# One core, attention and two expert layers: the gated sums are put together in another row, the weight work is spread one block a step, and two experts' second layer is turned

## The chip, the cores and the metric

The kernel runs on one core of one Trainium2 chip. The metric is the device time of one execution in microseconds (us). Three runs of the kernel before gave 814.67, 816.64 and 810.50 us, a median of 814.67. One profiled execution took 813.66 us; its trace spans 811.8 us from the first to the last instruction, with a granted TensorE clock of 0.996 on average.

## The reference

Three layers follow one another, all in fp32 and with outputs of 2304 tokens x 512:

```
x   = windowed attention(q, k, v)                     # 4 x 8 heads, 576 tokens, window 128, slopes on |i-j|
x   = (sigmoid(x @ w_gate) * (x @ w_val)) @ w_out     # 512 -> 1536 -> 512
idx = argmax(cosine(x, expert_emb) / tau)             # one of 8 experts a token
out[mask] = gate_w * (relu(x @ w1[e]) @ w2[e])        # 512 -> 1024 -> 512, for the tokens of expert e
```

## The kernel before, in words

An fp32 value is split in a high and a low part, and a product is three matmuls: high x high, low x high, high x low. The high part is a cast on ACT (`hi_copy`, L105), the low part a subtraction on DVE (`lo_sub`, L121).

**The gated layer.** The 512 -> 1536 product with the gate and value weights is done by Strassen's scheme for pairs of 512 tokens. The second pair (pair 1) is a loop of 12 steps f (L838 to L872), one block of 128 hidden rows a step. In a step PE runs seven products of six matmuls each, with names m1 to m7 and PSUM banks a, b and c, in this order: m5 (left operand S1, into c), m6 (S2, a), m1 of the next step (A11, a), m7 (S3, a), m2 of the next step (A12, b), m4 (A22, a), m3 (S4, c). Bank a has two buffers, so each product into it waits for an ACT copy of an earlier one: `r` at L535 and `c` at L527, L538 and L542. The sums of banks are made on DVE (L531, L539, L549). The same 512 x 512 tokens are later multiplied with w_out in Strassen's form too, so `keep_g` (L452 to L475) makes from four gated blocks (two steps f, an even and an odd one) the three of them that are used alone (A11, A12, A22) and the sums S1 to S4, and sends each by a DMA that POOL issues (L461) to DRAM. The gated value itself is the STT of L458 (a SCALAR_TENSOR_TENSOR on DVE), a sum is a TENSOR_TENSOR at L464. An even and an odd step share one tile `gq` with two halves, `low` and `high`.

**w_out's blocks.** w_out comes as 64-bit floats, 12 blocks of 128 rows (`wor`, 512 KB each, loaded by SP at L749). `split64` (L137) turns a block to fp32 in a row `cvwo`: one ACT instruction (L125), three on DVE (L131, L132, L134), a POOL DMA to DRAM (L141), then the cast on ACT (L105, named `wo`) and the subtraction on DVE (L121). A table WO_AT says in which step of pair 1 which block is converted.

**The rows of w_out and the route.** Then five rows of tokens (L1317, index i) go through w_out (`mm2`, L919), with Strassen's product in the middle. After each row the route to the experts is made: TensorE turns the rows, DVE copies them (`xT`, L960), TensorE multiplies with the expert vectors (`part`, L966; `lp`, L974). In rows i = 2 and 3 the weights of expert 0 are loaded and split (L1354 and L1355, tiles `wer`, `weh`, `wel`, eight parts).

**The experts.** The loop from L1431 runs experts 1 to 7. `ffn1` (L1121) makes the hidden rows with the weights stationary and the tokens moving; CAPS gives the columns: 384, 384, 384, 352, 320, 288, 256, 256 for e = 0 to 7. `ffn2` (L1139) has 128 tokens of the hidden rows as the stationary operand and moves 512 columns of weights, 24 matmuls for each tile of tokens; the last tile of e = 4 has 64 tokens, that of e = 5 has 32. DVE scales by the gate (L1143) and POOL scatters the rows to `out` (L1144). Between the tiles TensorE turns the gathered tokens of the next expert (`tx`, L1101, four transposes a tile).

**What sets the order.** Each engine has one queue and runs it in order. The order in a queue is set by a planner from modelled times, not by the program's text; a wait at the head of a queue holds everything behind it. Tiles of the kernel are rows of pools (33 rows in `bpool`, 10 in `mid`); a row that is used again waits for its last reader, a DMA too.

Of the kernel before, what the change touches and what calls it, by code (L numbers as in the profile page):

```python
# [9 lines left out]
F32 = mybir.dt.float32  # L10
# [50 lines left out]
def attn_ffn_moe(ctx: ExitStack, tc: tile.TileContext, qkd, vd, wgv, w_out, emb, tau, w1, w2, cst, ids, out):  # L61
# [381 lines left out]
        nc.sync.dma_start(gT_d[f * P:(f + 1) * P, t0:t0 + n], gate)  # L443

    NAMES = ["A11", "A12", "A22", "S1", "S2", "S3", "S4"]
    gq = {}

    def g7_rows(name, kk, n=1):
        r = (NAMES.index(name) * KF // 2 + kk) * P
# [2 lines left out]
    def keep_g(f, half, gate, val):  # L452
        kk, odd = divmod(f, 2)
        if not odd and kk not in gq:
            gq[kk] = slot([P, 2, 512], F32, f"gq{kk}")
        low, high = gq[kk][:, 0, :], gq[kk][:, 1, :]
        o = gate if odd else (low, high)[half]
        nc.vector.scalar_tensor_tensor(out=o, in0=gate, scalar=1.0, in1=val, op0=ALU.add, op1=ALU.mult)  # L458

        def put(name, t):  # L460
            nc.gpsimd.dma_start(g7_rows(name, kk), t)  # L461

        def sums(name, t, x, y, op):
            nc.vector.tensor_tensor(out=t, in0=x, in1=y, op=op)  # L464
            put(name, t)

        if odd or not half:
            put(f"A{half + 1}{odd + 1}", o)
        if not odd and not half:
            sums("S3", high, high, low, ALU.subtract)  # L470
        elif odd and half:
            sums("S2", high, o, high, ALU.add)
            sums("S1", low, high, low, ALU.add)
        elif odd:
            sums("S4", val, o, high, ALU.subtract)  # L475

    def piece(mm, ev):
        def both():
# [266 lines left out]
    def load_wo(j):  # L745
        if j >= KF:
            return
        t = slot([P, 1024], I32, f"wor{j}")
        nc.sync.dma_start(t, w_out[j].bitcast(I32))  # L749
        wo_raw[j] = t  # L750
# [57 lines left out]
    run(2)  # L808
    load_wt(1)
    load_wo(0)  # L810

    g_t = {}
    NB2 = 5
# [20 lines left out]
    sv[0]["m2"]()  # L834
    bB["S3+"]()
    bB["S3"]()
    WO_AT = {1: [0], 2: [1], 3: [2], 4: [3, 4], 5: [5], 6: [6], 7: [7, 8], 8: [9], 9: [10], 10: [11]}
    for f in range(KF):  # L838
        s, t = sv[f], sv[f + 1] if f + 1 < KF else None
        s["m5"]()  # L840
        if f == 0:
            bB["A22"]()
            bB["S4+"]()
        if f + 1 < NC:
            sum_w(f + 1, store=False)
        split_w(1, f + 1, 0)
        s["m6"]()
        if f == 0:
            bB["S4"]()
        if t:  # L850
            t["m1"]()
        s["m7"]()
        split_w(1, f + 1, 1)
        if t:
            t["m2"]()
        load_wt(f + 2)
        s["m4"]()
        for j in WO_AT.get(f, []):
            split_wo(j)
        for j in WO_AT.get(f + 2, []):  # L860
            load_wo(j)
        if f == KF - 1:
            split_g(ROWS[0], [0, 1])
        s["m3"]()
        if f == KF - 2:
            load_g(ROWS[0])
        if f == 7:
            load_emb()
        elif f == 9:
            norm_emb()  # L870
        elif f == 10:
            turn_emb()  # L872
# [257 lines left out]
    def ffn2(e, t, u, hs, idx, w=P):  # L1130
# [3 lines left out]
        for k in range(KE):  # L1134
# [3 lines left out]
            for h, ww in ((hh, wh), (hl, wh), (hh, wl)):  # L1138
# [5 lines left out]
        nc.gpsimd.indirect_dma_start(out=out, out_offset=IOA(ap=idx[0:w], axis=0), in_=y[0:w, :], in_offset=None,  # L1144
                                     bounds_check=NT - 1, oob_is_err=False)

    def tok_a(e, t):
        xh, xl = xe.pop(e)
        hr = op_.tile([P, FE], F32, tag="c", name=f"hr{e}_{t}")
        for z in range(2):  # L1150
            m = pt("s", f"ht{e}_{t}_{z}", 2)
            ds = slice(z * 512, (z + 1) * 512)
            cnt = 0
            for k in range(KD):
                wh, wl = wset[e][k]
                for x, w in ((xh, wh), (xl, wh), (xh, wl)):
                    nc.tensor.matmul(m, x[:, k, :], w[:, ds], start=(cnt == 0), stop=(cnt == 3 * KD - 1))
                    cnt += 1
            nc.scalar.activation(out=hr[:, ds], in_=m, func=AF.Relu)
        return hr  # L1160
# [142 lines left out]
    def sums_w2(lo, hi):  # L1303
        for kk in range(lo, hi):
# [5 lines left out]
            (1, 1): [lambda: sums_w2(3, 4), lambda: split_op(0)], (1, 2): [lambda: sums_w2(4, 5)],  # L1310
            (1, 3): [lambda: load_op(1), lambda: sums_w2(5, 6), lambda: split_w2(5), lambda: split_op(1)]}

    def more(i, z):
        for t in MORE.get((i, z), []):
            t()

    for i, b in enumerate(ROWS):  # L1317
        inner = {}
        if i == STRASSEN_AT:
            inner = strassen(late)  # L1320
        m = [pt("m", f"y{b}_{u}", 3) for u in range(2)]
        mm2(b, 0, 0, 4, m[0])
        if i and i != STRASSEN_AT:
            route_a(ROWS[i - 1], *late)
        for t in inner.get(0, []):
            t()
        more(i, 0)
        mm2(b, 0, 4, KF, m[0])
        for t in inner.get(1, []):
            t()  # L1330
        more(i, 1)
        mm2(b, 1, 0, 4, m[1])
        if i and i != STRASSEN_AT:
            route_b(ROWS[i - 1])
        for t in inner.get(2, []):
            t()
        more(i, 2)
        mm2(b, 1, 4, MT, m[1])
        if b == LATE[0]:
            close()  # L1340
        if b == LATE[1]:
            make_x(0, CE * P, True)
            for t in range(CE):
                transp(0, t, t)
        for t in inner.get(3, []):
            t()
        mm2(b, 1, MT, KF, m[1])
        if i + 1 < NB2 and i + 1 != STRASSEN_AT:
            split_g(ROWS[i + 1])
        if i >= STRASSEN_AT and i + 2 < NB2:  # L1350
            load_g(ROWS[i + 2])
        more(i, 3)
        late = route_x(b, m)
        for j in {2: (0, 1, 2, 3), 3: (4, 5, 6, 7)}.get(i, ()):  # L1354
            split_we(0, j, load_we(0, j), "a", "v")  # L1355

    def weights(e, lo=0, hi=NP):
        for j in range(lo, hi):
# [61 lines left out]
    def load_part(e, lo, hi):  # L1420
        if e < E:
            for j in range(lo, hi):
                raws[e, j] = load_we(order[e], j, e)
# [4 lines left out]

    gathers(2)
    load_part(2, 0, KD)  # L1430
    for e in range(1, E):  # L1431
        if e + 1 == E:
            tc.keep_in_program_order(nc.gpsimd.drain())
        load_part(e + 1, KD, NP)
        inner = {j + 1: [lambda e=e, j=j: convert(e + 1, j)] for j in range(KD)}
        if e == 1:
            inner[1].insert(0, lambda: ffn2(0, CE, 0, rest, col(0, CE)))
        t0 = EARLY[e] if e < len(EARLY) else 0
        hs = ffn1(e, CAPS[e] - t0 * P, between=inner)
        load_part(e + 2, 0, KD)  # L1440
        if e + 1 < E:
            make_x(e + 1, CAPS[e + 1])
        later = list(range(KD, NP))
        for t in tiles(e):
            if e + 1 < E and t in tiles(e + 1):
                transp(e + 1, t, t, width(e + 1, t))
            if t == tiles(e)[-1]:
                gathers(e + 2)
            if t >= t0:
                for j in later[:2]:  # L1450
                    convert(e + 1, j)
                later = later[2:]
                with tc.issue_after(latest(ENG.PE)[0]) if e + 1 == E else nullcontext():
                    ffn2(e, t, t - t0, hs, col(e, t), width(e, t))
# [117 lines left out]
```

## Time and profile before

| what | number |
|---|---|
| median of three runs | 814.67 us (810.50 to 816.64) |
| profiled execution, and its span | 813.66 us, 811.8 us |
| PE busy | 787.8 us, 97% of the span |
| DVE, ACT, POOL busy | 565.9 us (70%), 448.9 us (55%), 205.6 us (25%) |
| DMA over the span | 205 GB/s |
| stages: attention and first pair; pair 1; rows of w_out and Strassen; experts | to about 262; 262 to 392; to 555; to 812 us |

PE is busy 97% of the time, so a change counts through the gaps between matmuls and the number and spacing of the matmuls. Matmuls overlap: a row of the timeline shows the start and the duration of an instruction, and the spacing of starts is what a matmul costs PE; its duration is longer. Brackets give the idle time before an instruction and what ended it.

### The profile page before, as it was taken

To read this page: it belongs to the slowest core of one execution; us is meant where nothing else is said; L and a number is where in the kernel's file an instruction comes from. 1 tells how busy PE (TensorE), PEld (TensorE's weight loads), DVE (VectorE), ACT (ScalarE), POOL (GpSimd) and SP (SyncE) were. 2 spreads that over 40 slices of the span, in tenths; PEclk is the share of its full clock that TensorE was granted. 3 is DMA by queue.
4 is the path that set the end of the run, shared out by engine and by line. 5 is a ranking of instruction groups with operands and counts; after the bars stand their busy time and mean duration, and the time that the engine had idled before them with its cause. 6 is when DMAs were issued, how large, how long until landed. Compare 5 with 4: busy or idle time off the path is not lost. (4 is left out here: it accounts for less than half of the span.)

```text
span 811.8 us, 15640 instructions
## 1 busy us (share of the span) xinstructions
PE 787.8 (97%) x5562; PEld 652.3 (80%) x5563; DVE 565.9 (70%) x1430; ACT 448.9 (55%) x946; POOL 205.6 (25%) x330
## 2 busy tenths in 40 slices
PE   9989999999999999999999999999999999999997
PEld 5767878878888787778778877768789989879896
DVE  7988977777789887788679666746647554465621
ACT  6888766666556555456466587645445433344510
POOL 6856423322000022222310202422223021110200
PEclk9999999999999999999999999999999999999999
DMA  8687467765565789889946692232578364445100
GB/s 271 188 268 229 156 230 258 234 210 204 184 245 196 290 299 329 314 306 325 349 108 202 232 338 83 99 143 79 167 266 280 132 224 158 152 163 202 56 23 18
DMA packets 71070, 166.61 MB, mean 205 GB/s; under 512 B 9511, under 2 KB 23591, under 8 KB 70992
## 3 DMA queue, kind: packets, MB, share of 16 engines
q1 hardware_dynamic: 61136, 136.08, 50.1%
q0 software_dynamic: 9856, 29.53, 10.1%
q8 instruction: 44, 0.72, 0.4%
q14 instruction: 34, 0.28, 0.1%
HBM read 116.20 MB, written 50.03 MB: 205 GB/s over the span
## 5 line engine op out<-in xcount | busy, mean ns | idle before, releaser
L1121 PE MATMUL h<-xe,weh 128*128 128x256 f32 (+4 forms) x512 | 105.6, 300 | 0.2 <-DVE h L1124 0.2
L117 POOL TENSOR_SCALAR p<-p,rs 128x192 f32<-128x192 f32 x140 | 75.5, 557 | 103.7 <-DVE rs L268 53.3
L1139 PE MATMUL z<-weh,h 128*128 128x512 f32 (+3 forms) x320 | 101.5, 396 | 0.0
L121 DVE TENSOR_TENSOR wel<-wer,weh 128x1024 fp32r<-128x1024 f32 x64 | 77.1, 1220 | 18.3 <-ACT weh L105 6.1
L1121 PEld LDWEIGHTS h<-xe,weh 128*128 128x128 f32 x512 | 83.8, 189 | 1.7 <-DVE h L1124 0.8
L919 PE MATMUL y<-wo,gh 128*128 128x512 f32 x240 | 78.5, 399 | 0.0
L105 ACT CAST weh<-wer 128x1024 fp32r<-128x1024 f32 x64 | 66.5, 1048 | 21.3 <-DMA wer<-in_w 10.2
L252 ACT ACTIVATE p<-p,mx 128x192 f32<-128x192 f32 x144 | 64.0, 446 | 24.9 <-DVE mx L249 24.6
L1121 PE MATMUL h<-xe,wel 128*128 128x256 f32 (+4 forms) x256 | 76.6, 299 | 0.0
L1123 ACT ACTIVATE h<-h 128x256 fp32r<-128x256 f32 (+4 forms) x64 | 26.7, 417 | 79.3 <-PE h L1121 74.9
L1139 PEld LDWEIGHTS z<-weh,h 128*128 128x128 f32 (+3 forms) x320 | 56.4, 180 | 14.7 <-DVE sb_x L764 0.4
L1144 POOL DMA_INDIRECT out<-y,cols x19 | 22.2, 1169 | 169.6 <-DVE y L1143 147.0
L1139 PE MATMUL z<-wel,h 128*128 128x512 f32 (+3 forms) x160 | 62.7, 392 | 0.0
L1124 DVE SCALAR_TENSOR_TENSOR h<-h,h 128x256 fp32r<-128x256 f32 (+4 forms) x64 | 29.4, 463 | 44.6 <-ACT h L1123 44.6
L919 PEld LDWEIGHTS y<-wo,gh 128*128 128x128 f32 x240 | 44.7, 188 | 10.1 <-issue 1.6
L1143 DVE TENSOR_SCALAR y<-z,xg 128x512 f32<-128x512 f32 (+3 forms) x22 | 16.5, 748 | 48.8 <-PE z L1139 48.8
L1121 PEld LDWEIGHTS h<-xe,wel 128*128 128x128 f32 x256 | 48.6, 190 | 0.0
L919 PE MATMUL y<-wo,gl 128*128 128x512 f32 x120 | 47.1, 393 | 0.0
L461 POOL DMA_DIRECT2D g_d<-gq x24 | 13.5, 563 | 112.4 <-DVE gq L458 98.3
L1035 POOL DMA_INDIRECT tab_d<-ids_sb,ai x18 | 20.5, 1139 | 65.3 <-DVE xr L993 26.4
L238 PE MATMUL s<-qk 64*64 64x128 f32 (+2 forms) x864 | 35.2, 279 | 1.5 <-DVE mx L249 0.7
L249 DVE CUSTOM_DVE_ANT_0 p<-s,bias 128x192 f32<-128x192 f32 x96 | 30.7, 350 | 8.4 <-PE s L238 8.4
(470 smaller groups left out, 2111.2 us busy)
## 6 DMA issues: line engine op xcount, KB each, us to landing
wer<-in_w SPq DMA_DIRECT2D x64, 512.0 KB, 5.9
wr<-in_wgv SPq DMA_DIRECT2D x24, 512.0 KB, 5.5
qk<-in_qkd SPq DMA_DIRECT2D x36, 320.0 KB, 3.5
ol<-g_d SPq DMA_DIRECT2D x21, 512.0 KB, 6.1
gl<-gT_d SPq DMA_DIRECT2D x15, 512.0 KB, 8.3
v<-in_vd SPq DMA_DIRECT2D x36, 192.0 KB, 4.6
wor<-in_w_out SPq DMA_DIRECT2D x12, 512.0 KB
g_d<-gq POOLq DMA_DIRECT2D x24, 256.0 KB
```

Source lines behind the costliest of these rows:

```text
L105: nc.scalar.copy(o, i)
L117: nc.gpsimd.tensor_scalar(out=t, in0=t, scalar1=r, scalar2=0.0, op0=ALU.mult, op1=ALU.add)
L121: e.tensor_tensor(out=o, in0=i, in1=h.bitcast(F32), op=ALU.subtract)
L238: nc.tensor.matmul(ss[u][y * 64:(y + 1) * 64, j * WK + d:j * WK + d + n], q[halves[u], a:a + 64], k[halves[u], a + c0:a + c0 + n], start=T ...
L249: nc.vector.tensor_tensor_reduce(out=o, in0=ss[u][:, j * WK:(j + 1) * WK], in1=bias, scale=-0.125, scalar=3.0e38, op0=ALU.add, op1=ALU.min ...
L252: nc.scalar.activation(out=o, in_=o, func=AF.Exp, scale=-1.0, bias=mx[:, z:z + 1], accum_out=su[:, z:z + 1])
L919: nc.tensor.matmul(m, g[:, k % 4, u * P:(u + 1) * P], w[:, k % 3, :], start=(k == 0 and z == 0), stop=(k == KF - 1 and z == 2))
L1121: nc.tensor.matmul(m[:, :n], w[:, fs], x[:, k, :], start=(cnt == 0), stop=(cnt == 3 * KD - 1))
L1123: nc.scalar.activation(out=hh, in_=m[:, :n], func=AF.Relu)
L1124: nc.vector.scalar_tensor_tensor(out=hl, in0=m[:, :n], scalar=0.0, in1=hh.bitcast(F32), op0=ALU.max, op1=ALU.subtract)
L1139: nc.tensor.matmul(m[0:w, :], h, ww[:, ds], start=(cnt == 0), stop=(cnt == 3 * KE - 1))
L1144: nc.gpsimd.indirect_dma_start(out=out, out_offset=IOA(ap=idx[0:w], axis=0), in_=y[0:w, :], in_offset=None, bounds_check=NT - 1, oob_is_er ...
```

## The change

1. `keep_g`: the sum S2 of the odd step is no longer written over the half `high` of `gq` but over the row of the value (`val`, named `c`), S1 is made last, after S4, and S4 reads S2 from its new place.
2. The table WO_AT goes: step f converts block f and loads block f + 2, for f = 0 to 11. Before, nothing was converted at f = 0 and 11, two blocks each at f = 4 and 7, one at the other steps.
3. The eight weight parts of expert 0 are split one at a time, at points of the rows i = 3 and 4, instead of four at the end of row 2 and four at the end of row 3.
4. For the experts e = 4 and 5 the second layer is turned (`ffn2_across`): the weights are stationary in 128 x 128 blocks and the hidden tokens move, 320 or 288 columns, 4 x 24 = 96 matmuls in place of 72 of 512 columns. An ACT copy brings each quarter to SBUF; `rows_out` turns them back by 12 transposes an expert, in the next expert's `ffn1`, and then scales and scatters.

```diff
@@ keep_g
         elif odd and half:
-            sums("S2", high, o, high, ALU.add)
-            sums("S1", low, high, low, ALU.add)
+            s2[kk] = val
+            sums("S2", val, o, high, ALU.add)
         elif odd:
-            sums("S4", val, o, high, ALU.subtract)
+            sums("S4", val, o, s2[kk], ALU.subtract)
+            sums("S1", low, s2[kk], low, ALU.add)
@@ pair 1
     load_wo(0)
+    load_wo(1)
...
-    WO_AT = {1: [0], 2: [1], 3: [2], 4: [3, 4], 5: [5], 6: [6], 7: [7, 8], 8: [9], 9: [10], 10: [11]}
...
-        for j in WO_AT.get(f, []):
-            split_wo(j)
-        for j in WO_AT.get(f + 2, []):
-            load_wo(j)
+        split_wo(f)
+        load_wo(f + 2)
@@ expert 0's weights
+    def we0(j):
+        split_we(0, j, raw0.pop(j), "a", "v")
+        if j + 3 < NP:
+            raw0[j + 3] = load_we(0, j + 3)
+
+    for j, k in ((0, (3, 0)), (1, (3, 1)), (2, (3, 2)), (4, (4, 0)), (5, (4, 1)), (6, (4, 1)), (7, (4, 2))):
+        MORE[k] = MORE.get(k, []) + [lambda j=j: we0(j)]
...
-        for j in {2: (0, 1, 2, 3), 3: (4, 5, 6, 7)}.get(i, ()):
-            split_we(0, j, load_we(0, j), "a", "v")
+        if i == 2:
+            for j in range(3):
+                raw0[j] = load_we(0, j)
+        elif i == 3:
+            we0(3)
@@ experts
+    def ffn2_across(e, d, hs, yT):
+        n = CAPS[e]
+        m = pt("m", f"zt{e}_{d}", 3)
+        cnt = 0
+        for k in range(KE):
+            hh, hl = (h[k // 4][:, k % 4, :] for h in hs)
+            wh, wl = wset[e][KD + k // 2]
+            ds = slice((k % 2) * DM + d * P, (k % 2) * DM + (d + 1) * P)
+            for ww, h in ((wh, hh), (wh, hl), (wl, hh)):
+                nc.tensor.matmul(m[:, :n], ww[:, ds], h, start=(cnt == 0), stop=(cnt == 3 * KE - 1))
+                cnt += 1
+        nc.scalar.copy(yT[:, d, :], m[:, :n])
+
+    def rows_out(e, t, yT, idx, w):
+        q = pt("t", f"zr{e}_{t}", 2)
+        for d in range(KD):
+            nc.tensor.transpose(q[0:w, d * P:(d + 1) * P], yT[:, d, t * P:t * P + w], ident)
+        x = xg.pop((e, t))
+        y = row(f"y{e}_{t}")[:, 0:DM]
+        nc.vector.tensor_scalar_mul(y[0:w, :], q[0:w, :], x[0:w, DM:DM + 1])
+        nc.gpsimd.indirect_dma_start(out=out, out_offset=IOA(ap=idx[0:w], axis=0), in_=y[0:w, :], in_offset=None,
...
         inner = {j + 1: [lambda e=e, j=j: convert(e + 1, j)] for j in range(KD)}
+        inner[0], after = after, []
...
+        if e >= len(EARLY) and 0 < CAPS[e] % P <= P // 2:
+            yT = op_.tile([P, KD, CAPS[e]], F32, tag="c", name=f"yT{e}")
+            for d in range(KD):
...
+                convert(e + 1, KD + d)
+                ffn2_across(e, d, hs, yT)
+            after = [lambda e=e, t=t, y=yT: rows_out(e, t, y, col(e, t), width(e, t)) for t in tiles(e)]
+            continue
```

**DVE in pair 1, an odd step (f = 3), before.** The names: `c_3` are value and gate rows of step 3, `gq` the shared tile, `cvwo` the w_out block, `r_3` the row of the r copy.

```order
L458 SCALAR_TENSOR_TENSOR c_3_4269<-c_3_4269,c_3_4242 128x512
L131 TENSOR_SCALAR cvwo_4277<-cvwo_4277 128x512
L464 TENSOR_TENSOR gq_4187<-c_3_4269,gq_4187 128x512
L132 SCALAR_TENSOR_TENSOR cvwo_4277<-wor_4115,cvwo_4277 128x512
L464 TENSOR_TENSOR gq_4187<-gq_4187 128x512
L134 SCALAR_TENSOR_TENSOR cvwo_4277<-wor_4115,cvwo_4277 128x512
L549 TENSOR_TENSOR r_3_4225<-r_3_4225,c_3_4212 128x512
```

The same place after the change (its lines stand one further down from here on):

```order
L458 SCALAR_TENSOR_TENSOR c_3_4277<-c_3_4277,c_3_4250 128x512
L131 TENSOR_SCALAR cvwo_4285<-cvwo_4285 128x512
L464 TENSOR_TENSOR c_3_4250<-c_3_4277,gq_4197 128x512
L132 SCALAR_TENSOR_TENSOR cvwo_4285<-wor_4123,cvwo_4285 128x512
L550 TENSOR_TENSOR r_3_4233<-r_3_4233,c_3_4220 128x512
L134 SCALAR_TENSOR_TENSOR cvwo_4285<-wor_4123,cvwo_4285 128x512
L458 SCALAR_TENSOR_TENSOR c_3_4160<-c_3_4160,r_3_4233 128x512
L464 TENSOR_TENSOR gq_4197<-c_3_4250,gq_4197 128x512
```

S2, the first L464, is written to `c_3` and no longer to `gq`; the write to `gq`, which is S1 now, stands behind L134.

**ACT between steps 3 and 4, before.**

```order
L125 ACTIVATE cvwo_4277<-wor_4115 128x512
L105 CAST wh_5_4331<-wt_5_4261 128x1024
L105 CAST wo_0_4105<-cvwo_4277 128x512
L535 COPY r_4_4311<-a_4_4227 128x512
L527 COPY c_5_4320<-a_5_4313 128x512
```

After:

```order
L125 ACTIVATE cvwo_4285<-wor_4123 128x512
L536 COPY r_4_4321<-a_4_4235 128x512
L105 CAST wo_3_4283<-cvwo_4285 128x512
L528 COPY c_5_4330<-a_5_4323 128x512
L539 COPY c_4_4338<-a_4_4235 128x512
```

The cast of the block that an odd step converts now stands behind the r copy (steps 3, 5, 7 and 9); the casts of the even steps 2, 4, 6 and 8 stand ahead of the r copy of the step after, and that of step 1 too.

**DVE in the route of the row i = 4, before** (`sa_x`, `sb_x`: norms; `wel`: low parts of expert 0's weights).

```order
L121 TENSOR_TENSOR wel_6_6508<-wer_6_6505,weh_6_6507 128x1024
L761 TENSOR_SCALAR sa_x_6555<-sa_x_6555 128x2
L763 RECIPROCAL sb_x_6558<-sa_x_6555 128x2
...
L121 TENSOR_TENSOR wel_7_6514<-wer_7_6511,weh_7_6513 128x1024
L960 COPY xT_6532<-tl_0_6533 128x512
L960 COPY xT_6532<-tl_1_6539 128x512
```

After:

```order
L762 TENSOR_SCALAR sa_x_6537<-sa_x_6537 128x2
L764 RECIPROCAL sb_x_6540<-sa_x_6537 128x2
L959 COPY xT_6514<-tl_0_6515 128x512
L959 COPY xT_6514<-tl_1_6521 128x512
L765 TENSOR_TENSOR sb_x_6540<-sb_x_6540,ss_6486 128x2
L121 TENSOR_TENSOR wel_4_6571<-wer_4_6368,weh_4_6570 128x1024
L766 TENSOR_TENSOR sb_x_6540<-sb_x_6540,sa_x_6537 128x2
L121 TENSOR_TENSOR wel_5_6601<-wer_5_6410,weh_5_6600 128x1024
```

Both copies stand ahead of the four subtractions that this row makes.

## Rows read from the trace of the kernel before

**Rows 1.** Timeline of PE in pair 1: start, duration, engine, line, operation, idle before.

```profile
312.25 0.39 PE L438 MATMUL a<-xh_(1, 'A11')_3806,wdl 128*128 128x512 f32 x1
...
313.97 0.50 PE L438 MATMUL a<-xh_(1, 'S3')_3943,wh 128*128 128x512 f32 x1 [1.33 <-ACT r L535]
...
335.71 0.39 PE L438 MATMUL b<-xh_(1, 'A12')_3819,wdl 128*128 128x512 f32 x1
...
337.98 0.54 PE L438 MATMUL a<-xh_(1, 'A22')_3954,wh 128*128 128x512 f32 x1 [1.88 <-ACT c L538]
...
341.72 0.39 PE L438 MATMUL c<-xh_(1, 'S4')_3976,wdh 128*128 128x512 f32 x1
...
360.14 0.39 PE L438 MATMUL a<-xh_(1, 'A22')_3954,wt 128*128 128x512 f32 x1
...
361.79 0.50 PE L438 MATMUL c<-xh_(1, 'S4')_3976,wdh 128*128 128x512 f32 x1 [1.27 <-DVE c L539]
```

**Rows 2.** Timeline of DVE in pair 1.

```profile
333.80 0.69 DVE L464 TENSOR_TENSOR gq<-c,gq 128x512 f32<-128x512 f32 x1 [3.55 <-DMA g_d<-gq]
...
361.06 0.68 DVE L539 TENSOR_TENSOR c<-c,c 128x512 f32<-128x512 f32 x1
```

**Rows 3.** Timeline of POOL in pair 1: one put of S3.

```profile
325.53 0.54 POOL L461 DMA_DIRECT2D g_d<-gq  x1
```

**Rows 4.** Timeline of ACT in pair 1.

```profile
336.33 0.62 ACT L105 CAST wo<-cvwo 128x512 fp32r<-128x512 f32 x1 [3.69 <-DVE cvwo L134]
...
337.33 0.59 ACT L538 COPY c<-a 128x512 f32<-128x512 f32 x1
```

**Rows 5.** Timeline of ACT, two casts ahead of an r copy, and PE behind them.

```profile
292.14 0.62 ACT L105 CAST wo<-cvwo 128x512 fp32r<-128x512 f32 x1 [2.05 <-DVE cvwo L134]
...
293.00 0.39 PE L438 MATMUL a<-xh_(1, 'A11')_3806,wdl 128*128 128x512 f32 x1
293.30 0.50 PE L438 MATMUL a<-xh_(1, 'S3')_3943,wh 128*128 128x512 f32 x1
...
322.26 0.62 ACT L105 CAST wo<-cvwo 128x512 fp32r<-128x512 f32 x1 [1.17 <-DVE cvwo L134]
...
323.62 0.39 PE L438 MATMUL a<-xh_(1, 'S3')_3943,wh 128*128 128x512 f32 x1
```

**Rows 6.** Busy times by window: PE, PEld, DVE, ACT, POOL, PEclk, DMA share, GB/s.

```profile
337.00:343.00 6.00, 5.02 (x15) 4.02 (x16) 4.57 (x8) 3.54 (x6) 1.22 (x3) 0.72 0.93 287
```

**Rows 7.** Timeline of ACT, DVE and PE at the route of row 4.

```profile
539.80 1.05 ACT L105 CAST weh<-wer 128x1024 fp32r<-128x1024 f32 x1 [4.70 <-DMA wer<-in_w]
...
542.03 1.28 DVE L960 COPY xT<-tl 128x512 f32<-128x512 f32 x2
...
541.05 0.39 PE L919 MATMUL y<-wo,gl 128*128 128x512 f32 x1
...
543.37 0.64 PE L966 MATMUL part<-xT,enT 128*32 128x256 f32 x8 [1.93 <-DVE xT L960]
```

**Rows 8.** Timeline of PE in experts 4 and 5.

```profile
710.26 0.46 PE L1121 MATMUL h<-xe,weh 128*128 128x320 f32 x2
...
710.70 0.46 PE L1121 MATMUL h<-xe,weh 128*128 128x320 f32 x2
...
712.02 0.60 PE L1101 MATMUL tx<-cs,xg 128*128 128x128 f32 x4
...
712.38 0.71 PE L1139 MATMUL z<-weh,h 128*128 128x512 f32 x2
...
717.96 0.60 PE L1101 MATMUL tx<-cs,xg 128*128 128x128 f32 x4
...
741.48 0.43 PE L1121 MATMUL h<-xe,weh 128*128 128x288 f32 x2
...
741.88 0.43 PE L1121 MATMUL h<-xe,weh 128*128 128x288 f32 x2
```

**Rows 9.** PE by line and shape: busy, mean duration of one.

```profile
L1101 PE MATMUL tx<-cs,xg 128*128 128x128 f32 x76 | 11.3, 274 | 0.5 <-DVE xT L960 0.3 <-issue 0.2
```

## What the change will do to the time: the prediction

> **What bounds the kernel now.** I read the busy shares first. PE is busy 97% of the span, so a change pays through PE's gaps, or through the number and spacing of its matmuls. Then I read the list of what PE waits for, and the timeline of PE at each wait; for each wait I followed the timelines of the engines behind it back to the first thing that was late.
>
> Back to back, PE starts 24 matmuls of 512 columns in 5.58 us from 712.38 to 717.96 [rows 8], 0.23 each once the slower first one (some 0.1) is taken off. That is the measure for gaps. In pair 1 there are three real ones [rows 1]: 1.72 from 312.25 to 313.97, less 0.23, is 1.49; 2.27 from 335.71 to 337.98, less 0.23, is 2.04; 1.65 from 360.14 to 361.79, less 0.23, is 1.42. Behind the second the clock falls: in the window from 337 to 343 the mean granted clock is 0.72 [rows 6], a mixture of the levels 2.4 and 1.2 GHz, after PE had stood for 1.88 us. From 337.98 to 341.72 nine matmuls take 3.74 us, where nine times 0.23 is 2.07: 1.67 lost. In sum 6.6 us.
>
> All three have one root, and it shows in the dearest. DVE stands 3.55 us before the sum that it writes to `gq`, released by a DMA that reads `gq` [rows 2]. That DMA is S3's put, issued by POOL at 325.53 [rows 3]: it takes 8.3 us until DVE goes on at 333.80. Behind the sum in DVE's queue stand the w_out block's L132, the second sum, and L134. The block's cast on ACT waits for L134, 3.69 us [rows 4], and behind the cast stand the copies that free bank a: the one of L538 starts at 337.33, and PE goes on at 337.98 [rows 1]. The same holds at 312 to 314. In the third, the add of L539 that PE waits for comes at 361.06 [rows 2], behind S2's late write and the two blocks that f = 7 converts.
>
> At the route of row 4, PE stands 1.93 us for `xT`: 2.32 from 541.05 to 543.37, less 0.23, is 2.09 [rows 7]. ACT's cast of the last weight part of expert 0 waits 4.70 us for its load; its DVE subtraction is ahead of the `xT` copies, and these start at 542.03 only when it is over.
>
> **The change, part by part.**
>
> *S2 in another row.* The two sums, three adds and seven puts stay, as many and as large. S2 goes to a row that only DVE and ACT have touched, so DVE no longer waits for S3's put there. In DVE's new order the write into `gq` (S1, over A11) is three DVE instructions after L134, and the put it waits for is A11's, the step before. Counted in DVE instructions of some 0.6 us, it comes about 10.7 us after that put is issued; the put that I can time took 8.3 [rows 2, 3], so about 2.4 us of cover. If the cover goes, S1 waits and the low part of the w_out block, S4 and the next step's L540 behind it. The three gaps and the clock loss go: -6.6.
>
> *One block a step.* Same conversions, loads and puts; the doubled ones at f = 4 and 7 part. Block 0 in step 0 is hidden by the 9.5 us of PE's 42 matmuls a step. Block 11 goes to step 11; it is read first at the end of w_out's first row, and by the order it is ready some 2 us ahead: nothing, or a few tenths. What is new is where casts stand on ACT: in four steps (2, 4, 6, 8) the cast is ahead of the r copy. That form is in the trace: after the cast at 322.26 PE runs through at 323.62; after that at 292.14 the start at 293.30 comes 0.30 behind 293.00, and the next is slow by 0.11 more: 0.18 [rows 5]. Here a gated value stands ahead of L134 too, 0.6 us in place of another block's 0.34, so I take the middle: 4 x 0.1 = 0.4, between 0 and four times the cheapest gap of rows 1, 5.7. What is next in line is this cast. Pair 1 in sum: -6.2.
>
> *Expert 0's weights.* The same 8 loads, casts and subtractions. Three loads go out at the end of row 2, each next one when a part is split, on SP behind the same neighbours. The `xT` copies of rows 3 and 4 now stand ahead of the subtractions: -2.1. PE has fewer matmuls between turning the rows and `part` (5 of row 3 where 13 were, with the DVE copies of 1.28 [rows 7] between), so I put 0.2 at each of the two rows: between 0 and the 2.09 that went. In sum -1.7. The parts themselves are ready well before expert 0's first layer, at about 553.
>
> *The turned layers.* Before, three tiles of 24 matmuls: 72 x 0.23 = 16.6 us for each expert (the small third tile's stationary width saves nothing, since 512 columns move all the same). Now 96 matmuls with the weights stationary and 320 or 288 columns moving, which is just the form of the first layer: three in 0.44 (710.26 to 710.70), 0.147 each, and three in 0.40 (741.48 to 741.88), 0.133 each [rows 8], each with its own weight load. 96 x 0.147 = 14.1; 96 x 0.133 = 12.8. Twelve transposes an expert come on top: four take 0.36 (712.02 to 712.38 [rows 8]) and slow the next start by some 0.1, so 3 x 0.46 = 1.4. Expert 4: 14.1 + 1.4 - 16.6 = -1.1. Expert 5: 12.8 + 1.4 - 16.6 = -2.4. ACT gets four copies more, of some 0.4 us, while it is 55% busy; DVE's scalings are as many; both are hidden by 3.4 us of matmuls a quarter. The scatters come later, in the next expert's first layer, and the gathers of expert e + 2 go out one quarter before the end; the gathered rows are held longer, and one output row of `mid` waits for a freed one. I put 0.5 for the last quarter's copy and that row: -3.0, between -3.5 and 0.
>
> The Trainium skill, "TensorE: Matmul & The Clock Gate", section "Back-to-back issue gap", speaks against this part: it gives a sustained 81 ns a matmul at 128 columns and 131 at 512. On a straight line between them, an estimate, 320 columns would be 106, so 96 x 0.106 = 10.2 against 72 x 0.131 = 9.4, and the turned layer would lose 0.8 before its transposes. This trace has 0.147 and 0.23, so the rows decide.
>
> **Sum.** -6.2 - 1.7 - 3.0 = -10.9. From the profiled execution, 813.66, that is 802.8. The median shown is 1.0 above that execution; I take half of it: **803.3**.
>
> **Rivals.**
>
> *A. The wait moves (0.22).* DVE no longer waits, but the casts ahead of the r copies, or loads and puts that now collide in a stage where DMA is busy 0.93 of the time [rows 6], keep most of the gaps in pair 1. Then about 1.5 of its 6.2 is left: -1.5 - 1.7 - 3.0 = -6.2, and with a further 1 us for a late w_out block 11, -5.2: about 808.5. For it: ACT's queue is what PE hung on in two of three gaps. Against it: the two casts of that form, 0 and 0.18.
>
> *B. Slower (0.08).* A put that takes longer than 10.7 us. S1 then holds DVE as S2 did, now in each of the five odd steps from 3 on, since rows of `bpool` and halves of `gq` come round at that distance. Each would cost what the dearest did, 2.04 + 1.67 = 3.7; five are 18.6 in place of 6.6, +12.0; with -1.7 and -3.0 that is +7.3: about 821. It decides from the landing that exceeds 10.7 by more than the cover of the add L540, which is a few us. For it: DMA's share of 0.93. Against it: 8.3 measured in that very stretch, with no fewer transfers under way.
>
> *C. The turned layer gives nothing (0.06).* If transposes do not overlap, each costs its duration, 0.274 [rows 9]: 12 x 0.274 = 3.3 an expert where I have 1.4, 3.8 more for both; the sum is -7.1: 807. The Trainium skill, same page, "Part 4: PE-mode transpose", gives about 275 ns for one in a kernel's context, and the mean of rows 9 agrees as a duration. Against it: four start and finish in 0.36 before the next matmul starts [rows 8], so it is no spacing.
>
> *D. More than forecast (0.06).* The last step's and the first step's small gaps in pair 1 go with the new block order and the waits I have added don't come: -6.6 - 2.1 - 3.5 = -12.2 and 1 more: about 800, and below with a run as far under the median as the 810.5 of before.
>
> **How the numbers follow.** The forecast's case has 0.58, and holds between 800 and 806.5. A measurement of this kernel can tell about 1%, that is 806.5 and 822.8 around the median. Faster by over 1%: the forecast, D, and a small part of C, 0.64, less a little for the spread of runs: 0.63. Within 1%: A and the rest of C, some of B: 0.30. Slower: 0.07. The range is 798 to 811: down to D with such a run, up over A and C; B and the outer parts of A are left out.
>
> **What would show it.** Right: no DVE wait of more than 0.5 us for a put ahead of S2; a clock of 1.00 through all of pair 1; PE's waits there shrunk to the first and last step; `xT` not behind a subtraction at row 4; PE starts of 0.147 and 0.133 in experts 4 and 5's second layer. Wrong: S1 released by a DMA, with L540 late behind it (B); PE released by the r copy behind a cast at several even steps (A); the transposes' starts 0.27 apart (C); a wait of the first rows' matmuls for w_out's last block, or of the gates' loads, that starts earlier than its data.

## The result, and the profile after

The changed kernel takes 803.69 us (median of six runs, 802.94 to 804.63), the kernel before 814.48 in six runs of that comparison: a ratio of 0.9869, with a 95% interval of 0.9841 to 0.9897. The forecast was 803.3 in a range of 798 to 811. The profiled execution after, the fastest of its six, took 802.94 us with a span of 800.7; against 813.66 of before that is -10.72, where the sum said -10.9.

Starts of the same matmuls in both traces cut the span into stretches (us):

| stretch | before | after | difference | forecast |
|---|---|---|---|---|
| start to the first matmul of step 0 of pair 1 | 268.96 | 268.02 | -0.94 | 0 |
| step 0, to the first matmul of step 1 | 7.82 | 9.16 | +1.34 | 0 |
| from there to the last matmul of pair 1 | 114.95 | 108.40 | -6.55 | -6.2 |
| from there to the last of w_out's rows | 160.96 | 159.16 | -1.80 | -1.7 |
| from there to the kernel's last matmul | 253.21 | 249.93 | -3.28 | -3.0 |

So in this pair of executions three terms came at their sizes, a gap that the forecast did not have stands in step 0, and the early part, whose work is the same, happened to give back most of it. Other executions share the gain out otherwise, as the section on why the prediction was right shows.

The timeline of DVE after, in the odd step that answers to [rows 2]: S2 is the first L464, S1 the second.

```profile
328.63 0.68 DVE L464 TENSOR_TENSOR c<-c,gq 128x512 f32<-128x512 f32 x1
...
330.43 0.69 DVE L134 SCALAR_TENSOR_TENSOR cvwo<-wor,cvwo 128x512 int32<-128x512 int32 x1
...
331.63 0.69 DVE L464 TENSOR_TENSOR gq<-c,gq 128x512 f32<-128x512 f32 x1
```

No bracket: neither waits for a DMA, where S2 stood 3.55 us before. A11's put, which S1 overwrites, was issued 10.5 us ahead (POOL, timeline):

```profile
321.10 0.54 POOL L461 DMA_DIRECT2D g_d<-gq  x1 [5.97 <-DVE gq L458]
```

The timeline of ACT shows both places of the cast: behind the r copy for an odd step's block, ahead of it for an even one's.

```profile
311.85 0.59 ACT L536 COPY r<-a 128x512 f32<-128x512 f32 x1 [2.92 <-PE a L438]
312.33 0.63 ACT L105 CAST wo<-cvwo 128x512 fp32r<-128x512 f32 x1
...
321.44 0.62 ACT L105 CAST wo<-cvwo 128x512 fp32r<-128x512 f32 x1 [2.00 <-DVE cvwo L134]
321.96 0.58 ACT L536 COPY r<-a 128x512 f32<-128x512 f32 x1
```

The second form costs what the forecast's dearer row did [rows 5]. PE, timeline, at the same place two steps earlier: 0.29 from 303.06 to 303.35 and a slow next start, 0.18 in all.

```profile
303.06 0.39 PE L438 MATMUL a<-xh_(1, 'A11')_3806,wdl 128*128 128x512 f32 x1
303.35 0.50 PE L438 MATMUL a<-xh_(1, 'S3')_3945,wh 128*128 128x512 f32 x1
303.69 0.39 PE L438 MATMUL a<-xl_(1, 'S3')_3946,wh 128*128 128x512 f32 x1
```

By windows (PE, PEld, DVE, ACT, POOL, PEclk, DMA share, GB/s), pair 1 is granted the full clock throughout, with the DMA engines as busy as before (0.88 in that window):

```profile
262.00:392.00 130.00, 127.43 (x558) 102.52 (x558) 108.24 (x171) 69.68 (x108) 31.70 (x58) 1.00 0.90 320
```

PE's waits of more than 0.3 us in pair 1 are down to three: 0.68 in step 0 and 0.72 in the last step, which before has too, and a new one in step 0. There, in the timeline of PE, 275.23 less 273.75 less 0.23 is 1.25, for a low part of the weights that DVE makes.

```profile
273.75 0.39 PE L438 MATMUL b<-xl_(1, 'A12')_3820,wh 128*128 128x512 f32 x1
275.23 0.50 PE L438 MATMUL a<-xh_(1, 'A11')_3806,wt 128*128 128x512 f32 x1 [1.09 <-DVE wt L121]
```

At the route of row 4, DVE copies `xT` as soon as the rows are turned, and the last part of expert 0 comes 6.8 us behind it; its cast still waits for a load, now to nobody's cost. DVE, then ACT, then PE, which starts `part` without a wait (against [rows 7]):

```profile
528.79 1.27 DVE L959 COPY xT<-tl 128x512 f32<-128x512 f32 x2
...
535.63 1.23 DVE L121 TENSOR_TENSOR wel<-wer,weh 128x1024 fp32r<-128x1024 f32 x1 [1.01 <-issue]
```

```profile
534.55 1.05 ACT L105 CAST weh<-wer 128x1024 fp32r<-128x1024 f32 x1 [2.37 <-DMA wer<-in_w]
```

```profile
530.15 0.64 PE L965 MATMUL part<-xT,enT 128*32 128x256 f32 x8
```

And PE in the turned layers, to set beside [rows 8]: three matmuls in 0.44 at 320 columns (704.85 to 705.29), in 0.40 at 288 (734.58 to 734.98), and the last four transposes of expert 4, 0.38 until the next matmul starts.

```profile
704.85 0.46 PE L1155 MATMUL zt<-h,weh 128*128 128x320 f32 x2
...
705.29 0.46 PE L1155 MATMUL zt<-h,weh 128*128 128x320 f32 x2
...
722.61 0.29 PE L1120 MATMUL h<-xe,wel 128*128 128x288 f32 x1
722.89 0.63 PE L1162 MATMUL zr<-cs,yT 128*64 128x128 f32 x4
723.27 0.51 PE L1120 MATMUL h<-xe,weh 128*128 128x288 f32 x2
...
734.58 0.43 PE L1155 MATMUL zt<-h,weh 128*128 128x288 f32 x2
...
734.98 0.43 PE L1155 MATMUL zt<-h,weh 128*128 128x288 f32 x2
```

The transposes of the third tile come 0.28 behind the matmul ahead of them, 0.15 over its spacing; what holds them there the trace does not show. The forecast had allowed 0.5 at such places.

### The profile page after: what moved, and what is told of

Read it like the earlier page. It is cut to its first block, busy times and chain, and to the rows that moved or that the text cites. A ratio compares the mean times of both kernels' runs of the same rounds, so it can differ in the third digit from the quotient of the medians.

```text
span 800.7 us, 15794 instructions
## 1 busy us (share of the span) xinstructions
PE 781.1 (98%) x5635; PEld 655.8 (82%) x5635; DVE 565.9 (71%) x1430; ACT 452.5 (57%) x954; POOL 204.8 (26%) x330
## 5 line engine op out<-in xcount | busy, mean ns | idle before, releaser
L1138 PE MATMUL z<-weh,h 128*128 128x512 f32 (+1 forms) x224 | 71.3, 396 | 0.0
L1123 DVE SCALAR_TENSOR_TENSOR h<-h,h 128x256 fp32r<-128x256 f32 (+4 forms) x64 | 29.4, 463 | 43.1 <-ACT h L1122 43.0
L1138 PEld LDWEIGHTS z<-weh,h 128*128 128x128 f32 (+1 forms) x224 | 40.8, 186 | 9.0 <-DVE sb_x L765 0.4
L1138 PE MATMUL z<-wel,h 128*128 128x512 f32 (+1 forms) x112 | 43.8, 391 | 0.0
L1143 POOL DMA_INDIRECT out<-y,cols x13 | 14.5, 1115 | 109.4 <-DVE y L1142 101.2
L461 POOL DMA_DIRECT2D g_d<-gq x18 | 10.0, 555 | 113.0 <-DVE gq L458 111.7
L1142 DVE TENSOR_SCALAR y<-z,xg 128x512 f32<-128x512 f32 (+1 forms) x16 | 12.0, 749 | 35.9 <-PE z L1138 35.9
```

The costliest lines, as they stand in the source:

```text
L1123: nc.vector.scalar_tensor_tensor(out=hl, in0=m[:, :n], scalar=0.0, in1=hh.bitcast(F32), op0=ALU.max, op1=ALU.subtract)
L1138: nc.tensor.matmul(m[0:w, :], h, ww[:, ds], start=(cnt == 0), stop=(cnt == 3 * KE - 1))
```

## The experiments

"Stretch" is the one from the first matmul of step 1 to the last of pair 1, 114.95 before and 108.40 after. A step of PE starts with its m5; what DVE and ACT do for a step f reaches PE while it is in step f + 1. Each ratio is to the runs of the kernel before in the same comparison, with its 95% interval.

### The first part alone

```diff
-            sums("S2", high, o, high, ALU.add)
-            sums("S1", low, high, low, ALU.add)
+            s2[kk] = val
+            sums("S2", val, o, high, ALU.add)
         elif odd:
-            sums("S4", val, o, high, ALU.subtract)
+            sums("S4", val, o, s2[kk], ALU.subtract)
+            sums("S1", low, s2[kk], low, ALU.add)
```

> Only the first part: S2 over the value's row, S1 last; the table of w_out blocks stays. Theory (S2's wait for S3's put is the root of the three gaps in pair 1): the gaps at steps 3 and 5 and the half clock behind the second go, 5.2 us; the third, at step 7 with its two blocks, goes or keeps up to 1.4. The stretch from the first matmul of step 1 to the last of pair 1, 114.95 in before, becomes 108.4 to 109.9; run about 808 to 809. Rival (the doubled w_out blocks make the gaps): no gap goes, stretch 114 to 115, run about 814.

Measured: 814.43 us, ratio 0.9989 (0.9963 to 1.0015): nothing, where 808 to 809 were expected, and a stretch of 112.21, between the theory's and the rival's. Up to step 7 the theory holds to the tenth: from the first matmul of step 1 to that of step 7 it takes 60.48 us in place of 65.64, -5.16, and no DVE row waits for a put of `gq`. Behind that, where the two blocks of step 7 are converted, 2.7 of it is taken back (steps 7 to 9: 33.06 in place of 30.39). PE stands at 352.24 for the r copy of ACT:

```profile
350.23 0.39 PE L438 MATMUL a<-xh_(1, 'A11')_3806,wdl 128*128 128x512 f32 x1
352.24 0.50 PE L438 MATMUL a<-xh_(1, 'S3')_3943,wh 128*128 128x512 f32 x1 [1.62 <-ACT r L536]
```

and ACT, in its timeline, stood 5.45 us for a load of weights before it came to that copy:

```profile
348.53 1.05 ACT L105 CAST wh<-wt 128x1024 fp32r<-128x1024 f32 x1 [5.45 <-DMA wt<-tf_d]
349.48 0.63 ACT L533 ACTIVATE c<-c 128x512 f32<-128x512 f32 x1
350.01 0.58 ACT L543 ACTIVATE c<-a 128x512 f32<-128x512 f32 x1
350.49 1.22 ACT L125 ACTIVATE cvwo<-wor 128x512 f32<-128x512 f32 x2
351.61 0.58 ACT L536 COPY r<-a 128x512 f32<-128x512 f32 x1
```

SP issued that load at 340.19, after it had issued nothing for 9 us:

```profile
330.73 0.32 SPq L398 DMA_DIRECT2D wdh<-wq_d  x1
339.77 0.32 SPq L398 DMA_DIRECT2D wdl<-wq_d  x1
340.19 0.38 SPq L403 DMA_DIRECT2D wt<-tf_d  x1
```

The kernel before issues the same load at 340.26, but its PE is 5.6 us later at step 8, so that cost nothing there. The changed kernel has such a pause too (7.1 us) and issues the load at 338.63, 8.8 us ahead of its step 8, where it is 6.2 here. The rest of the gain goes between there and Strassen's first matmul (0.5) and at the route of row 4: from Strassen's first matmul to the last of w_out's rows it takes 3.8 us more. The experiment with the fourth part alone shows the same there.

### The second part alone

```diff
+    load_wo(1)
...
-        for j in WO_AT.get(f, []):
-            split_wo(j)
-        for j in WO_AT.get(f + 2, []):
-            load_wo(j)
+        split_wo(f)
+        load_wo(f + 2)
```

> Only the second part: one w_out block a step; S2 still goes over the half of gq that S3's put reads. Theory: DVE still waits 2 to 4 us for that put in the odd steps, with a block now in each of them behind it; the stretch from step 1 to the end of pair 1 stays at 113 to 118 (before 114.95), run 813 to 818. Rival (doubled blocks make the gaps): stretch 108.4 to 109.5, run about 808.

Measured: 815.00 us, ratio 1.0004 (0.9980 to 1.0028), as expected, and a stretch of 112.84, just under the expected 113 to 118. DVE waits for S3's put in five odd steps, 0.70 to 2.34 us, for instance

```profile
292.11 0.69 DVE L464 TENSOR_TENSOR gq<-c,gq 128x512 f32<-128x512 f32 x1 [1.87 <-DMA g_d<-gq]
...
333.61 0.69 DVE L464 TENSOR_TENSOR gq<-c,gq 128x512 f32<-128x512 f32 x1 [2.34 <-DMA g_d<-gq]
```

and behind the first of them PE stands 1.81 us for an r copy, a gap that before had not. Step 0 takes 9.17 here too: the new gap of the changed kernel comes with this part. The doubled blocks alone are not the cause either. Each of these two parts by itself gives nothing that can be measured in the median; in the changed kernel, which has both, the stretch is 108.40.

### The third part alone

```diff
-        for j in {2: (0, 1, 2, 3), 3: (4, 5, 6, 7)}.get(i, ()):
-            split_we(0, j, load_we(0, j), "a", "v")
+        if i == 2:
+            for j in range(3):
+                raw0[j] = load_we(0, j)
+        elif i == 3:
+            we0(3)
```

(with `we0` and its table as in the change).

> Only the third part: expert 0's weights split one by one. Theory: the gap of 2.1 us ahead of part at row 4 goes, nothing comes in its place: PE from the first matmul of w_out's rows to the first of expert 0 is 1.8 us shorter than before's 164.8, run about 812.8. Rival (the wait goes to the other row's part, or to lp): 0 to 0.5 us shorter, run about 814.4.

Measured: 809.65 us, ratio 0.9946 (0.9928 to 0.9965). In the trace the stretch that was named takes 163.18 where before takes 164.84: -1.66, as expected. The median falls by more, 5.3. The next experiment shows where that can come from. The stretch in pair 1, whose code is that of before, is 113.32 in this trace.

### The fourth part alone

```diff
+        if e >= len(EARLY) and 0 < CAPS[e] % P <= P // 2:
+            yT = op_.tile([P, KD, CAPS[e]], F32, tag="c", name=f"yT{e}")
+            for d in range(KD):
...
+                ffn2_across(e, d, hs, yT)
```

> Only the fourth part: the second layers of experts 4 and 5 turned. Theory (price by spacing of starts: 0.147, 0.133 and 0.23 a matmul, four transposes 0.46): from the first 320-column matmul to the last matmul of the kernel 3.2 us less than before's 107.95, run about 811.4. Rival (transposes cost their duration, 0.274 each): 0 to 0.5 more, run about 814.6 to 815.

Measured: 810.93 us, ratio 0.9961 (0.9939 to 0.9983). From the first 320-column matmul to the last matmul 104.75 in place of 107.95: -3.20, as expected. Pair 1, whose code is that of before, has smaller gaps here: the stretch is 111.79 (113.32 with the third part alone), so its waits for puts change from execution to execution: the longest is 2.02 us here and 3.55 in the trace of before. And the gap at row 4, whose code is also that of before, is dearer. PE stands 2.13 us there:

```profile
537.55 0.39 PE L919 MATMUL y<-wo,gl 128*128 128x512 f32 x1
540.07 1.02 PE L966 MATMUL part<-xT,enT 128*32 128x256 f32 x8 [2.13 <-DVE xT L960]
```

and then the granted clock is lower, 0.85 from 533 to 556, first row, where before had 1.00 behind its 1.93 us, second row, from the other trace:

```profile
533.00:556.00 23.00, 20.56 (x106) 15.83 (x104) 8.00 (x33) 8.75 (x18) 6.27 (x7) 0.85 0.34 126
```

```profile
533.00:556.00 23.00, 20.75 (x124) 16.77 (x123) 9.99 (x40) 10.58 (x21) 7.20 (x8) 1.00 0.34 126
```

From the first matmul of w_out's rows to the last it takes 167.89 here, 164.62 in the trace of before and 162.80 after. So the gap costs 1.8 us in one execution and 5.1 in another, by the clock behind it; the kernel with only the first part had 0.85 in that window too, the one with only the second part 1.00. The granted clocks of all runs fit the third part's 5.3 in the median: their mean is 0.9938 in the 31 runs of before in that comparison and 0.9971 in the ten of the third part alone. That is, as an estimate, 0.0033 x 812 = 2.7 us of the full clock, beside the gap of 2.1 itself. In which stretch the clock fell in runs without a trace is not known.

### Step 0: one load moved

```diff
     load_wo(0)
-    load_wo(1)
...
         split_wo(f)
+        if f == 0:
+            load_wo(1)
         load_wo(f + 2)
```

> The changed kernel with one line moved: the load of w_out's block 1 is issued in step 0 instead of ahead of pair 1. In the planner's order the sum for S3 (L331) then stands again ahead of the gated value of the first pair (L442) on DVE, as in before. Theory (that swap makes the new gap of 1.26 us in step 0 of the changed kernel): the gap goes, and the rest stays; from the first matmul of step 0 to that of step 1 7.8 us in place of 9.16, run about 802.4. Rival (block 0's conversion in step 0 makes the gap): 9.1 stays, run about 803.7.

Measured: 802.00 us, ratio 0.9853 (0.9815 to 0.9891). Step 0 takes 7.79 us in place of 9.16, and the matmul that waited goes on in its spacing:

```profile
273.72 0.40 PE L438 MATMUL b<-xl_(1, 'A12')_3820,wh 128*128 128x512 f32 x1
273.95 0.40 PE L438 MATMUL a<-xh_(1, 'A11')_3806,wt 128*128 128x512 f32 x1
```

Block 0 is still converted in step 0, so the place of the load makes the gap, through the planner: with the load issued up front it put a gated value of the first pair (L442) ahead of the sum for S3 (L331) on DVE. The timeline of DVE in the changed kernel,

```profile
264.77 0.69 DVE L442 SCALAR_TENSOR_TENSOR c<-c,c 128x512 f32<-128x512 f32 x1 [1.33 <-ACT c L543]
...
266.10 1.22 DVE L331 TENSOR_TENSOR xq_(1, 'S3')_3943<-xf,xf 128x1024 f32<-128x1024 f32 x1
```

and with the load in step 0:

```profile
263.33 1.22 DVE L331 TENSOR_TENSOR xq_(1, 'S3')_3941<-xf,xf 128x1024 f32<-128x1024 f32 x1
264.73 0.69 DVE L442 SCALAR_TENSOR_TENSOR c<-c,c 128x512 f32<-128x512 f32 x1 [0.19 <-ACT c L543]
```

The sum comes 2.8 us earlier, since it need not stand behind a value that waits 1.33 us for ACT. That this swap alone, of all that the planner may have moved, carries the 1.4 us was not tested by itself.

### Two blocks at an even step

```diff
-    WO_AT = {1: [0], 2: [1], 3: [2], 4: [3, 4], 5: [5], 6: [6], 7: [7, 8], 8: [9], 9: [10], 10: [11]}
+    WO_AT = {1: [0], 2: [1], 3: [2], 4: [3, 4], 5: [5], 6: [6], 7: [7], 8: [8], 9: [9], 10: [10], 11: [11]}
```

(with the other three parts of the change).

> The changed kernel with blocks 0 to 11 in steps 1 to 11, two of them at step 4, an even one. Theory (once S2 waits for nothing, a doubled block costs nothing in step 4; what hurts in the first-part-only kernel is the one at step 7, whose second load takes a row of bpool and lets the next weights' load start late): no gap over 0.3 between steps 1 and 10; from the first matmul of step 1 to the last of pair 1 107.5 to 109, no gap of 1.26 in step 0; run 802 to 803.5. Rival (any doubled block costs 1.5 to 4 us now): stretch 110 to 112.5, run 804 to 806.5.

Measured: 802.17 us, ratio 0.9850 (0.9811 to 0.9888), a stretch of 108.36, 7.79 for step 0, and no gap over 0.3 in steps 1 to 10. So doubling as such costs nothing once S2 waits for no put; with the one at step 7 gone, the gaps that the first part alone had behind that step are gone too. Why it hurts stays open: the expected reason was that its second load takes a row of the pool from the weights' load, and SP's pause fits that, but the changed kernel has a pause too, and no run shows the row by itself.

### Transposes twice

```diff
             for d in range(KD):
-                nc.tensor.transpose(q[0:w, d * P:(d + 1) * P], yT[:, d, t * P:t * P + w], ident)
+                for _ in range(2):
+                    nc.tensor.transpose(q[0:w, d * P:(d + 1) * P], yT[:, d, t * P:t * P + w], ident)
```

> The changed kernel with every transpose of rows_out done twice, 24 more in all. Theory (a transpose costs its spacing, 0.36 us for four): from the first 320-column matmul to the kernel's last, 104.8 in the changed kernel, 2.2 us more, run about 805.9. Rival (it costs its duration, 0.274): 6.6 us more, run about 810.3.

Measured: 805.66 us, ratio 0.9888 (0.9850 to 0.9926). The experts' stretch is 107.19 in place of 104.77: +2.42 for 24 transposes, 0.10 each. PE shows the 24 of expert 4 in 2.70 us, from 721.95 to 724.65:

```profile
721.95 2.94 PE L1163 MATMUL zr<-cs,yT 128*128 128x128 f32 x24
724.65 0.51 PE L1120 MATMUL h<-xe,weh 128*128 128x288 f32 x2
```

The Trainium skill, "TensorE: Matmul & The Clock Gate", "Part 4: PE-mode transpose", has about 275 ns in a kernel's context; as a duration that agrees with [rows 9], as a price in a stream it does not.

### The put late, first try

```diff
-        if odd or not half:
+        if odd:
             put(f"A{half + 1}{odd + 1}", o)
+        if odd and half:
+            nc.gpsimd.dma_start(g7_rows("A11", kk), low)
```

> The changed kernel with A11's put issued in the odd step, some 1.5 us ahead of S1's write over it, where the changed kernel has 10.5 us. Theory (the put's landing takes about 8 us and is hidden in the changed kernel; without its cover S1 holds DVE): DVE waits 5 to 8 us for that put in each of the six odd steps, and PE 2 to 5 us behind it, with the half clock now and then; the stretch from the first matmul of step 1 to the last of pair 1 goes from 108.4 to 120 to 138, run 815 to 833. Rival (nothing that PE needs stands behind S1 on DVE): stretch 108 to 110, run about 804.

Measured: 803.02 us, ratio 0.9855 (0.9817 to 0.9892), a stretch of 108.45. This says nothing about the theory: POOL still issues the put in the even step, at 321.81. The order of POOL's queue is the planner's, and the edit did not change the put's lead.

### The put late, behind S2

```diff
             sums("S2", val, o, high, ALU.add)
+            nc.vector.scalar_tensor_tensor(out=low, in0=val, scalar=0.0, in1=low, op0=ALU.mult, op1=ALU.add)
+            put("A11", low)
```

(and A11 not put in the even step).

> The changed kernel with A11 written once more by DVE behind S2 (zero times S2 added, 0.6 us a pair of steps) and put only then, so that the planner cannot issue the put earlier: about 3 us ahead of S1's write over it, where the changed kernel has 10.5. Theory (the put takes some 8 us to land, and only the lead hides it; the add L540 behind S1 is what PE waits for): DVE waits 4 to 6 us in each odd step, PE 2 to 5 us behind it, with the half clock now and then; the stretch from the first matmul of step 1 to the last of pair 1, 108.4 in the changed kernel, becomes 120 to 140, run 815 to 835. Rival (what stands behind S1 is not needed in time by PE): stretch 108.4 to 111, run 804 to 806.5.

Measured: 814.40 us, ratio 1.0007 (0.9986 to 1.0028), a stretch of 120.16, +11.8: just inside the expected stretch, the run just under the expected one. DVE's waits for that put are five, 0.62 to 3.04 us, where 4 to 6 were expected. The put is issued at 292.13 by POOL, and DVE goes on at 298.42, 6.3 us later, having stood 3.04; PE, through the add that the forecast named, 2.35, and then the starts are 0.42 and more apart, at a granted clock of 0.59 from 300 to 303.

```profile
292.13 0.54 POOL L461 DMA_DIRECT2D g_d<-gq  x1 [0.66 <-DVE gq L474]
```

```profile
298.42 0.69 DVE L464 TENSOR_TENSOR gq<-c,gq 128x512 f32<-128x512 f32 x1 [3.04 <-DMA g_d<-gq]
```

```profile
300.36 0.68 PE L438 MATMUL c<-xh_(1, 'S4')_3978,wdh 128*128 128x512 f32 x1 [2.35 <-DVE c L542]
300.84 0.63 PE L438 MATMUL c<-xl_(1, 'S4')_3979,wdh 128*128 128x512 f32 x1
301.26 0.63 PE L438 MATMUL c<-xh_(1, 'S4')_3978,wdl 128*128 128x512 f32 x1
```

PE's list of waits has this five times, 8.1 us in sum. So without the lead of that put the run is as slow as before: the lead is worth as much as the whole change gains. The edit also gives DVE one more instruction of 0.6 us in each pair of steps, whose own cost was not measured; the waits themselves are all ended by the put.

### Expert 3 turned too

```diff
-        if e >= len(EARLY) and 0 < CAPS[e] % P <= P // 2:
+        if e >= len(EARLY) and 0 < CAPS[e] % P:
```

> The changed kernel with expert 3's second layer (352 tokens) turned as well. Theory (price by spacing of starts: 96 matmuls at 0.161 and three times 0.46 for the transposes, 15.5 + 1.4 = 16.9, against 72 at 0.23, 16.6): from the first 352-column matmul to the first 320-column one, 33.5 in the changed kernel, and from there to the last, 104.8, in sum 0.3 us more; run about 804. Rival (the turned form gains at any width under 384, by the columns saved alone: 3 x 512 x 24 against 4 x 352 x 24, 8%): 1.2 us less, run about 802.5.

Measured: 804.19 us, ratio 0.9877 (0.9842 to 0.9912). From the first 352-column matmul to the last it takes 139.32 where the changed kernel takes 138.30: +1.02 and not -1.2, so the price by spacing decides. The 0.7 beyond the expected 0.3 is one wait in expert 3's first layer, ahead of the turned work. PE waits for a DVE row (L1123, 664.18), which waits 2.92 us for ACT; ACT starts at 663.68, having stood 2.98, and the trace names nothing of the kernel that ended it. Its cause is open:

```profile
664.76 0.59 PE L1120 MATMUL h<-xe,weh 128*128 128x352 f32 x2 [0.72 <-DVE h L1123]
```

### The better version beside the changed kernel

> The changed kernel once more, on the same chip as the next run, for the comparison: about 803.5.

> The changed kernel with the load of w_out's block 1 in step 0, once more beside the changed kernel. Theory: 1.3 to 1.4 us less than the changed kernel, the gap in step 0. Rival (the difference of the two lone runs was their chips' and days'): 0 to 0.5 less.

Measured on one chip: 803.42 us (802.79 to 804.99) for the changed kernel, ratio 0.9868 (0.9843 to 0.9893); 801.62 (800.95 to 804.04) with the load of block 1 in step 0, ratio 0.9851 (0.9824 to 0.9879). The medians lie 1.8 apart, nearer the theory's 1.3 to 1.4 than the rival's, but the intervals overlap; what the traces show is step 0, 9.17 and 7.79. It is the fastest version here, 12.3 us under before's 813.90 in that comparison.

## Why the prediction was right, and where it was not

- **S2 in another row: right in mechanism, wrong in "one root", and its size is that of one execution.** The forecast put all three gaps down to S3's put. For the first two that is shown: -5.16 with the first part alone, and no wait of DVE for a put of `gq`. The third belongs to the doubled block of step 7: with S2's wait gone and the doubling left, other waits take its place, and the run is no faster. Since the change has both parts, the term came at -6.55 for -6.2 against the trace of before. Two more traces have before's code in pair 1, with 113.32 and 111.79; against the mean of the three, 113.35, the term is -5.0. One small reading was off: by the order shown, S1 stands two DVE instructions behind L134 and not three, and the lead came at 10.5 for 10.7.
- **One block a step.** The casts ahead of r copies cost 0.13 to 0.18 each; 0.1 was put in. "Hidden in step 0" was right of the block, which costs nothing there when the load is issued in the step; the +1.34 comes from the load of block 1 ahead of pair 1, by way of the planner's new order on DVE, between two instructions that the diff does not name. The forecast had no term for it. The early part, -0.94, covered it by luck: in the changed kernel's second profile that part takes 269.68, 1.66 more than in the first.
- **Expert 0's weights: right in mechanism, too small.** -1.80 for -1.7 in the pair of traces. In the median of runs it is worth 5.3 by itself. The forecast counted the gap alone, since its one trace has the full clock behind it (1.00 from 533 to 556). Over the four traces that have before's code there (before, and the first, second and fourth part alone) the stretch from the end of pair 1 to the last of w_out's rows is 160.96, 165.53, 161.02 and 164.23, a mean of 162.9, and the term is -3.8 against it.
- **The turned layers.** -3.28 for -3.0; -3.20 by themselves. Spacing of starts was the right price, for matmuls (0.147 and 0.133 again) and transposes (0.10). The rule of the Trainium skill's section "Back-to-back issue gap" (page "TensorE: Matmul & The Clock Gate"), 81 to 131 ns, would have made this part a loss; the trace after has its matmuls where the trace before had them.
- **The rivals.** A did not come. In the kernel with the first part alone something like it did: an r copy came late on ACT, behind a load of weights, and more than half of pair 1's gain was lost; its 814.4 is not to be set against A's 808.5, which has the gains of the third and fourth parts in it. B is real as a mechanism: where the put's lead is taken away, five gaps come back in the odd steps, as it said, behind the add it named. Its price was too high: 3.7 for each, 18.6 in all, where the five with their clock cost 11.8, so the kernel is as slow as before and not 7 us slower. It did not come, since 10.5 us of lead cover the landings: the waits give 6.3 and 8.3, and where the traces record the landing of a put of `gq` it is 6.3 to 8.8 in the changed kernel and 2.6 to 9.1 with the first part alone. C is ruled out by the doubled transposes.
- **The sum over one execution.** It used the sizes of one trace. Other executions of the same code had 3 us less in pair 1 and 3 us more at the route. Against the means above the change gives about -5.0 in pair 1 and -3.8 at the route, in place of -6.2 and -1.7: the first term was too large and the second too small by about as much, so that the sum came within 0.2 is in part luck. The changed kernel's runs lie closer together (802.8 to 805.0 in the last comparison, before 811.3 to 818.5). Why is not shown: with the first part alone no DVE row waits for a put of `gq`, and its runs still go from 811.1 to 818.4; the ten runs of the third part alone, without the gap at row 4, go from 808.3 to 812.0.

## What to carry to other kernels

When an engine waits for a DMA to finish reading a buffer, look for a write that can go to a buffer no DMA reads, and count the lead that the next such write has: the same puts cost 11.8 us with 3 us of lead and nothing with 10.5. Price a change of matmul shape by the spacing of starts of that very shape elsewhere in the trace, never by durations. And a fix that gives nothing alone may be half of one: follow where the time is taken back before you drop it, and compare the queues' orders even in places that the diff does not name.

## What the hardware showed that was not expected

The same gap of about 2 us ahead of `part` left the granted clock at 1.00 in the traces of before (1.93 us) and of the second part alone (2.08); in those of the first (2.01) and of the fourth part alone (2.13) it was followed by a mean of 0.85 from 533 to 556, a mixture of 2.4 and 1.2 GHz. In the latter that made it 5.1 us instead of 1.8. The length of the gap does not tell the two apart, since 2.08 kept the clock and 2.01 did not; what does is open.
